# Output matmuls for two batches on a block-diagonal slot matrix, and small filler matmuls ahead of them, in a gated recurrence with a soft mixture of experts

## The chip, the cores and the metric

The kernel runs on one core of a Trainium2 chip. The metric is the device time of one execution in microseconds (us). A core has five engines that run at the same time, each with its own queue of instructions in program order: TensorE (PE in the profile; its loads of the stationary operand are the row PEld), VectorE (DVE), ScalarE (ACT), GpSimd (POOL) and SyncE (SP). TensorE writes to PSUM, eight banks of 2 KB per partition; other engines copy from there to SBUF, and DMA engines move data between SBUF and the memory (HBM). In this kernel SP issues the loads of the inputs and all stores, GpSimd the loads of the expert weights.

## What is computed

```python
def _attn_ref(x, f_logit, lower_bound):             # x, f_logit: 4 x 5056 x 256
    sig = 1.0 / (1.0 + np.exp(-f_logit))
    f = lower_bound[None, None, :] + (1.0 - lower_bound[None, None, :]) * sig
    i = 1.0 - f
    for t in range(S):
        h = f[:, t] * h + i[:, t] * x[:, t]
        y[:, t] = h

def _moe_ref(x, phi, w1, w2):                       # x: 20224 x 256, 8 experts with 4 slots each
    logits = x @ phi                                # 20224 x 32
    d = softmax over the tokens (logits)
    slot_input = d.T @ x                            # 32 x 256
    for e in range(E):
        h = np.maximum(slot_input[e] @ w1[e], 0.0)  # w1[e]: 256 x 1024
        slot_out[e] = h @ w2[e]                     # w2[e]: 1024 x 256
    c = softmax over the slots (logits)
    return c @ slot_out                             # 20224 x 256
```

The result of the recurrence is the token matrix of the mixture. No output row can be written before the last token of every batch has passed through the recurrence, because `slot_input` sums over all tokens. The output is 20224 x 256 in float32, 20.7 MB.

## The kernel before, in words

**First part, the recurrence (0 to about 134 us).** The 5056 tokens of a batch are cut into 10 groups of 512; a unit is one group of one batch, 40 in all. A unit is loaded, gated with a sigmoid (ScalarE), multiplied (GpSimd), transposed to channels (TensorE), scanned along the tokens (DVE, line 250), transposed back (line 263), and its logits against `phi` are taken. The exponentials of the logits stay in SBUF as `etall`: a tile of 128 partitions by 5056 tokens in bfloat16, where partitions 32b to 32b+31 hold the 32 slots of batch b. The order of the instructions is written out by hand; the framework adds the waits, and follows a tile for that, so that two parts of one tile may count as one.

**Second part, the experts (134 to 147 us).** TensorE is the only engine with much to do. In order: `slot_ps` is finished (lines 341 and 390); three matmuls of `spin` (line 130), which multiply the first 128 columns of `w1_sb[0]` with its first 512 columns into an unused bank, `tail[:, 1]`, and whose results nobody reads; four transposing matmuls of `slot_sb` (line 514); three more of `spin`; the first layer of the experts (line 544) into `hi_ps`; transposes of it (line 559); the second layer for experts 0 to 3 into `so4_ps` (line 580); then for experts 4 to 7 into `so_ps`, eight matmuls for each expert with `wide` as stationary operand (line 590). After the eight of expert 4 stand one matmul pair that adds `so4`, and the row sums (lines 324 and 327): 23 matmuls with a stationary part of `etall` and the four columns of `ones`, which give the denominators of the softmax over slots for the later blocks; DVE turns them into `rrow` (lines 600 and 601). The 24 matmuls of experts 5 to 7 follow. Line 602 then scales `so_ps` by `rcs` into `slot_out` (128 x 256, bfloat16; the rows of batch b again at partitions 32b to 32b+31, with the same 32 rows for all batches).

**Third part, the output (from 147 us).** The tokens of a batch are cut into `blocks`: two of 2048 tokens (16 rows of 128 partitions each), one of 896 (7 rows), and 64 left over that `rest` treats. For one row of one batch, `share` (line 620) makes one matmul: stationary is the part of `etall` with the 32 slots of this batch and 128 tokens, moving is `slot_out` with 256 columns.

```python
nc.tensor.matmul(op[:, j], ew[:, :, r + j], slot_out[ds(b * NS, NS), :],
                 start=True, stop=True, skip_group_check=True)
```

The result in PSUM (`op`, up to four rows of 256 columns, two banks) is scaled by `rrow` into `ob` in SBUF, in turn by DVE (`by_vector`, one instruction for four rows, line 610) and by ScalarE (`by_scalar`, one instruction a row, line 614). `pieces` does this for the first block of batch 0 in small parts, each stored as soon as it is ready (line 646); `whole` does a block of one batch and stores it with one DMA (line 657). The order is: `pieces` for block 0 of batch 0, `whole` for the block of 896 tokens for each batch, `rest`, then `whole` for the seven blocks of 2048 tokens. SP issues the stores in this order, and waits at each for the copies that fill it. `ob` is a pool of six buffers of 16 KB a partition, `op` one of four buffers of two banks.

Of the kernel before, what the change touches and what calls it, by code (L numbers as in the profile page):

```python
# [9 lines left out]
F32 = mybir.dt.float32  # L10
# [8 lines left out]
def kernel(  # L19
# [10 lines left out]
    nc = tc.nc  # L30
# [66 lines left out]
    for j in range(B // 2):  # L97
        nc.vector.memset(pair_ones[ds(j * 2 * NS, 2 * NS), ds(j, 1)], 1.0)

    def lb_constants():  # L100
        nc.vector.tensor_scalar(omlb, lb, -1.0, 1.0, ALU.mult, ALU.add)
        nc.vector.tensor_scalar(nomlb, lb, 1.0, -1.0, ALU.mult, ALU.add)
# [12 lines left out]
    nc.vector.memset(csum, 0.0)  # L115
    w1_r = moe_w1.rearrange("e (p o) f -> e p o f", o=DC)
    w2_r = moe_w2.rearrange("e (p fc) d -> e p fc d", p=P)
    w1_sb = [store.tile([P, DC, F], BF16, name=f"w1_sb{e}") for e in range(E)]
    w2_sb = [store.tile([P, FC, D], BF16, name=f"w2_sb{e}") for e in range(E)]

    def load_w(i):
        if i < E:
# [2 lines left out]
            nc.gpsimd.dma_start(out=w2_sb[i - E], in_=w2_r[i - E])  # L125


    def spin(dst, k):
        for _ in range(k):
            nc.tensor.matmul(dst, w1_sb[0][:, 0, :P], w1_sb[0][:, 0, :G],  # L130
                             start=True, stop=True, skip_group_check=True)

    W_AT = {9: 1, 15: 1, 21: 1, 27: 1, 31: 1, 33: 1, 34: 3, 35: 1, 36: 6}
    w_next = [0]
    ctx.enter_context(tc.manual_schedule())

    held = ExitStack()
    psu = held.enter_context(tc.tile_pool(name="psu", bufs=2, space=PSUM))
    psp = held.enter_context(tc.tile_pool(name="psp", bufs=1, space=PSUM))
    ld = held.enter_context(tc.tile_pool(name="ld", bufs=3))  # L140
    with tc.tile_pool(name="sp2", bufs=3) as sp2, \
# [271 lines left out]
        for n in range(n_unit):  # L413
            if n < SINGLE - 2:
                if n:
                    unit(to_tokens, n - 1)
                    unit(u_to_channels, n + 1)
                s_to_channels(n + 2)
                gate(n + 3, 1 if n + 3 < SINGLE else 2)
                decay(n + 2, 1)  # L420
                if n % 2 == 0:
                    unit(load, n + AHEAD)
                unit(enter, n + 3)
            else:
                end = n >= n_unit - 6
                if n % 2 == 0:
                    unit(load, n + AHEAD)
                    if n == SINGLE - 2:
                        to_tokens(n - 1)
                        keep_tokens(n - 1)  # L430
                    if not end:
                        unit(gate, n + 4)
                else:
                    unit(decay, n + 1)
                    if n == n_unit - 5:
                        gate(n + 3)
                        exps(odd - 1)
                if not end and n != n_unit - 7:
                    group(exps, n - 2)

                unit(enter, n + 3)
                for _ in range(W_AT.get(n, 0)):
                    load_w(w_next[0])
                    w_next[0] += 1

                if n == n_unit - 2:
                    unit(u_to_channels, n + 1)
                if n != SINGLE - 2:
                    unit(to_tokens, n - 1)
                if n == n_unit - 2:  # L450
                    keep_tokens(n - 1)
                if n % 2 == 0:
                    unit(s_to_channels, n + 2)
                    unit(s_to_channels, n + 3)
                if n != n_unit - 2:
                    unit(u_to_channels, n + 1)
                if n in (n_unit - 5, n_unit - 4):
                    idle(4)
                if n == n_unit - 2:
                    tail = psp.tile([P, 2, G], F32, name="tail", tag="sp")  # L460
                    rs_ps = tail[:, 0, ds(0, n_grp * R * B)].rearrange(
                        "p (q b) -> p q b", b=B)
                    late_ps, odd_ps = (
                        tail[:, 1].bitcast(BF16)[:, ds(i * R * P, R * P)].rearrange(
                            "p (r s) -> p r s", r=R) for i in range(2))
                    logits(odd)
                    exps(odd)
                    slots(odd - 1)
                    spin(tail[:, 1], 1)
                    odd_weights()  # L470
                elif not end:
                    group(logits, n - 1)
            if n == n_unit - 1:
                logits(last, [0, 1, 2])
                late_exps([0, 1, 2])
                row_sums(0)
                late_weights([0, 1, 2], nc.scalar.copy)

            unit(scan, n)
            if n == 0:  # L480
                rep_constants()
            if n not in (SINGLE - 2, n_unit - 2):
                unit(keep_tokens, n - 1)
            if n == n_unit - 3:
                weights_to_tokens(odd - 1)
                slots(odd - 2)
            elif not n >= n_unit - 6:
                group(weights_to_tokens, n - 3)
                batch(slots, n - 4, 0)
                batch(slots, n - 4, 1)  # L490
# [13 lines left out]
        slots(odd)  # L504
        late_slots([0, 1, 2])
        late_slots([3])
        spin(tail[:, 1], 3)
        slot_sb = hpool.tile([P, G, DC], BF16, name="slot_sb", tag="h")
        slot_sb = slot_sb.rearrange("p t o -> p (t o)").bitcast(F32)[:, ds(0, D)]
        nc.vector.tensor_copy(slot_sb, slot_ps)  # L510
# [3 lines left out]
            nc.tensor.matmul(sin_ps[:, o], slot_v[:, o], rep[:, 0],  # L514
                             start=True, stop=True, skip_group_check=True)

    slot_out = store.tile([P, D], BF16, name="slot_out")
    with tc.tile_pool(name="ew", bufs=1) as ew, \
         tc.tile_pool(name="pm", bufs=2, space=PSUM) as pm, \
         tc.tile_pool(name="pbig", bufs=1, space=PSUM) as pbig:  # L520

        rep2 = rep.rearrange("p b s -> p (b s)")

        spin(tail[:, 1], 3)
        sin = ew.tile([P, DC, NS], BF16, name="sin")
        nc.vector.tensor_scalar_mul(sin[:, 0], sin_ps[:, 0], omlb[:, ds(0, 1)])
        nc.scalar.activation(sin[:, 1], sin_ps[:, 1], ACT.Copy, scale=omlb[:, ds(1, 1)])
# [24 lines left out]
            his.append(hi)  # L552
        cs_ps = pm.tile([P, 1], F32, name="cs_ps", tag="pm")
        rcs = ew.tile([P, 1], F32, name="rcs")
        for q in range(E // Q):
            ht_ps = psu.tile([P, FC, P], BF16, name="ht_ps", tag="up")
            hi_v = his[q].rearrange("p (c f) -> p f c", f=FC)
# [2 lines left out]
            if q == 0:  # L560
                nc.tensor.matmul(cs_ps, rep2, cs1, start=True, stop=True)
                src = ht_ps.rearrange("p f (j s) -> p f j s", s=NS)[:, :, :, ds(0, SPE)]
                src = bass.AP(tensor=src.tensor, offset=src.offset,
                              ap=[list(src.ap[0]), [P, FC], [NS + SPE, Q], [1, SPE]])
                dst = hid[:, :, :, ds(0, SPE)]
                dst = bass.AP(tensor=dst.tensor, offset=dst.offset,
                              ap=[list(dst.ap[0]), [Q * NS, FC], [NS + SPE, Q], [1, SPE]])
                nc.scalar.copy(dst, src)
                nc.vector.reciprocal(rcs, cs_ps)
                continue  # L570
            for j in range(Q):
                s0 = (Q + j) * SPE
# [15 lines left out]
        for j in range(Q):  # L588
# [5 lines left out]
            if j == 0:  # L594
                nc.tensor.matmul(so_ps, rep2, so4, start=False, stop=False,
                                 skip_group_check=True)
                for i in range(1, len(blocks)):
                    row_sums(i)
                q = n_grp * R - 1
                nc.vector.reciprocal(rrow[:, wide_r:q], rs_ps[:, wide_r:q])  # L600
                nc.vector.reciprocal(rrow[:, q, ds(0, B // 2)], rs_ps[:, q, ds(0, B // 2)])
        nc.vector.tensor_scalar_mul(slot_out, so_ps, rcs)


    held.close()
    with tc.tile_pool(name="pout", bufs=4, space=PSUM) as pout, \
         tc.tile_pool(name="osb", bufs=6) as osb:

        def by_vector(ob, op, scale):
            nc.vector.tensor_tensor(ob, op, scale.broadcast_to(list(ob.shape)), ALU.mult)  # L610
# [5 lines left out]
        def share(op, i, b, r, k):  # L616
            t0, n_r = blocks[i]
            ew = etall[ds(b * NS, NS), ds(t0, P * n_r)].rearrange("s (p r) -> s p r", r=n_r)
            for j in range(k):
                nc.tensor.matmul(op[:, j], ew[:, :, r + j], slot_out[ds(b * NS, NS), :],  # L620
                                 start=True, stop=True, skip_group_check=True)

        def scale_of(i, b, r, k):
# [24 lines left out]
        def whole(i, b):  # L648
# [7 lines left out]
                by(ob[:, ds(r, k)], op[:, ds(0, k)], scale_of(i, b, r, k))  # L656
            nc.sync.dma_start(out=rows_of(i, b), in_=ob)

        def rest():
            n_p = B // 2  # L660
            op = pout.tile([P, R, D], F32, name="op", tag="op")
            ob = osb.tile([P, n_p, D], F32, name="ob", tag="ob")
            for j in range(n_p):
                k = ds(j * 2 * NS, 2 * NS)
                nc.tensor.matmul(op[:, j * R // n_p], left[k].rearrange("s t u -> s (t u)"),
                                 slot_out[k, :], start=True, stop=True, skip_group_check=True)
            by_vector(ob, op.rearrange("p (j k) d -> p k j d", j=n_p)[:, 0],
                      rrow[:, n_grp * R - 1, ds(0, n_p)].unsqueeze(2))
            dst = out.rearrange("(b t) d -> t b d", b=B)
            for j in range(n_p):  # L670
                nc.sync.dma_start(out=dst[ds(S - L, L), ds(2 * j, 2)], in_=ob[:, j])

        end = len(blocks) - 1
        pieces(0, 0, [(1, 2), (3,), (2,)])
        for b in range(B):
            whole(end, b)
        rest()
        for i in range(end):
            for b in range(B):
                if i or b:  # L680
                    whole(i, b)


# [28 lines left out]
```

## Time and profile before

| what | value |
|---|---|
| median of 12 runs | 203.84 us (203.2 to 205.33) |
| profiled execution | 203.79 us, span 202.0 us |
| busy in the span | PE 130.9, DVE 144.6, ACT 137.2, POOL 99.2 us |
| read and written | 58.23 MB read, 20.71 MB written, 391 GB/s over the span |
| mean granted TensorE clock | 0.836 |
| output matmuls, line 620 | 156, of 32x128 stationary and 256 moving columns |
| output copies | ACT line 614: 76, mean 491 ns; DVE line 610: 23, mean 1104 ns |
| stores of 2 MB | 7, median 15.9 us from issue to landing |

The span runs from the first to the last instruction of the profiled execution; the time of the execution is 1.79 us longer. Busy times of engines overlap, so they don't add up to the span. A matmul's own duration in the profile contains its way through the array, and neighbours overlap; what one costs in a row of many is the distance between them. The row "PEclk" gives the clock that TensorE was granted in tenths of full speed (9 is 90% or more).

### The profile page before, as it was taken

The numbers are of one execution on the slowest core, as the hardware profiler recorded it, in microseconds if no ns is written. First come the engines' busy times: TensorE is split into PE (matmuls) and PEld (weight loads), VectorE is DVE, ScalarE is ACT, GpSimd is POOL, SyncE is SP. The second block draws the span as 40 slices with busy tenths as digits, with TensorE's granted clock in tenths as the row PEclk, the third lists the DMA queues.
The fourth block names the chain that finished last, engine by engine and source line by source line (L and its number), as shares of the span: only waits on it lengthen the run. The fifth ranks groups of instructions, "written<-read, shape, count | busy, mean of one in ns | idle before, by whom it ended". The sixth has DMA issues, their size and how long they took to land.

```text
span 202.0 us, 3056 instructions
## 1 busy us (share of the span) xinstructions
PE 130.9 (65%) x1097; PEld 102.0 (50%) x1097; DVE 144.6 (72%) x162; ACT 137.2 (68%) x193; POOL 99.2 (49%) x70
## 2 busy tenths in 40 slices
PE   0586473874976658584976776999989999910000
PEld 0365342754864556564766555665965766700000
DVE  1699888698799999979998799915268887710000
ACT  2688664899988999599996498434069799940000
POOL 2588585893979469952995859950000000000000
PEclk9999999699699999879997999999985555555555
DMA  6999999999999999999999999999539999999993
GB/s 176 416 406 413 406 412 408 404 414 309 416 409 380 345 414 407 321 409 396 390 310 406 324 245 211 213 212 217 110 135 397 421 422 435 422 415 428 444 425 162
DMA packets 17614, 70.74 MB, mean 350 GB/s; under 512 B 2096, under 2 KB 3120, under 8 KB 16704
## 3 DMA queue, kind: packets, MB, share of 16 engines
q1 hardware_dynamic: 15120, 62.13, 76.8%
q0 software_dynamic: 2336, 8.42, 20.7%
q8 instruction: 8, 0.13, 0.2%
q14 instruction: 6, 0.05, 0.1%
q10 hardware_dynamic: 144, 0.00, 0.0%
HBM read 58.23 MB, written 20.71 MB: 391 GB/s over the span
## 4 chain that ended last, share of the span: by engine, by line
PE 30%; DVE 26%; DMA 15%; ACT 9%; issue 7%; SPq 1%; ACTq 0%; DVEq 0%
DVE h L250 20%; DMA f_t<-in_f_logit_dram 11%; PE op L620 9%; ACT ob L614 5%; PE hp L263 5%; DVE ht L277 4%; DMA x_t<-in_x_dram 4%; PE sp L217 4%; PE so_ps L590 2%; ACT s_t L191 2%; PE up L217 2%; PE tail L324 1%; SPq L181 1%; PE slot_ps L341 1%; PE hi_ps L544 1%
## 5 line engine op out<-in xcount | busy, mean ns | idle before, releaser
L202 POOL TENSOR_TENSOR u_t<-s_t,x_t 128x1024 bf16<-128x1024 bf16 (+1 forms) x39 | 82.4, 2130 | 29.9 <-ACT s_t L191 22.4
L250 DVE TENSOR_TENSOR_SCAN h<-a,h,up 128x512 bf16<-128x512 f32 (+1 forms) x72 | 86.4, 1250 | 6.2 <-PE up L217 3.8
L263 PE MATMUL hp<-ident_f,h 128*128 128x128 f32 (+1 forms) x160 | 31.2, 322 | 32.8 <-DVE ht L277 19.8
L191 ACT ACTIVATE s_t<-f_t 128x2048 bf16<-128x2048 f32 (+2 forms) x23 | 38.4, 1670 | 16.0 <-DMA f_t<-in_f_logit_dram 15.9
L240 ACT ACTIVATE a<-sp,nomlb 128x1024 f32<-128x1024 bf16 (+2 forms) x46 | 43.3, 993 | 3.5 <-PE sp L217 1.9
L263 PEld LDWEIGHTS hp<-ident_f,h 128*128 128x128 f32 (+1 forms) x160 | 23.1, 208 | 42.7 <-DVE ht L277 24.5
L614 ACT ACTIVATE ob<-op,rrow 128x256 f32<-128x256 f32 x76 | 28.6, 491 | 8.9 <-PE op L620 8.5
L217 PE MATMUL sp<-ident_f,s_t 128*128 128x128 f32 x144 | 23.9, 315 | 9.6 <-ACT s_t L191 6.1
L620 PE MATMUL op<-slot_out,etall 32*128 32x256 bf16 x156 | 28.2, 400 | 1.9 <-ACT ob L614 0.9
L610 DVE TENSOR_TENSOR ob<-op,rrow 128x1024 f32<-128x1024 f32 (+3 forms) x23 | 24.4, 1104 | 5.8 <-PE op L620 4.5
L217 PEld LDWEIGHTS sp<-ident_f,s_t 128*128 128x128 f32 x144 | 19.8, 164 | 11.1 <-issue 6.0
L620 PEld LDWEIGHTS <-etall 32*128 32x128 bf16 x156 | 20.2, 154 | 9.5 <-issue 4.5
L217 PE MATMUL up<-ident_f,u_t 128*128 128x128 f32 x144 | 24.0, 292 | 0.6 <-POOL u_t L202 0.6
L217 PEld LDWEIGHTS up<-ident_f,u_t 128*128 128x128 f32 x144 | 18.7, 154 | 1.8 <-POOL u_t L202 1.0
L277 DVE COPY ht<-hp 128x512 f32<-128x512 f32 (+1 forms) x22 | 14.8, 670 | 3.1 <-PE hp L263 3.0
L277 ACT COPY ht<-hp 128x512 f32<-128x512 f32 (+1 forms) x18 | 10.4, 576 | 4.9 <-PE hp L263 4.9
L250 DVE TENSOR_TENSOR_SCAN h<-a,up 128x512 bf16<-128x512 f32 x8 | 9.3, 1207 | 0.7 <-PE up L217 0.7
L291 PE MATMUL lg<-h,phi 128*32 128x512 bf16 (+1 forms) x80 | 6.9, 391 | 0.0
L341 PE MATMUL slot_ps<-ht,et 128*32 128x256 bf16 (+1 forms) x144 | 5.7, 277 | 0.8 <-DVE et L315 0.8
L191 ACT ACT_TABLE_LOAD x4 | 5.1, 1283 | 1.2 <-PEq L696 1.2
L300 ACT ACT_TABLE_LOAD x4 | 5.1, 1283 | 0.1
L300 ACT ACTIVATE etall<-lg 128x1024 bf16<-128x1024 f32 (+1 forms) x5 | 4.6, 927 | 0.0
(88 smaller groups left out, 90.0 us busy)
## 6 DMA issues: line engine op xcount, KB each, us to landing
f_t<-in_f_logit_dram SPq DMA_DIRECT2D x36, 512.0 KB, 10.5
x_t<-in_x_dram SPq DMA_DIRECT2D x36, 512.0 KB, 10.7
out_dram<-ob SPq DMA_DIRECT2D x7, 2048.0 KB, 15.9
w_sb<-in_moe_w_dram POOLq DMA_DIRECT2D x16, 512.0 KB, 8.4
out_dram<-ob SPq DMA_DIRECT2D x4, 896.0 KB, 7.9
f_t<-in_f_logit_dram SPq DMA_DIRECT2D x4, 384.0 KB, 7.7
x_t<-in_x_dram SPq DMA_DIRECT2D x4, 384.0 KB, 7.4
out_dram<-ob SPq DMA_DIRECT2D x4, 256.0 KB, 3.8
```

Source lines behind the costliest of these rows:

```text
L191: nc.scalar.activation(s_t, f_t, ACT.Sigmoid, scale=-1.0)
L202: nc.gpsimd.tensor_tensor(uts[n][:, :r], s_t[:, :r], x_t[:, :r], ALU.mult)
L217: nc.tensor.transpose(ps[:, :, r], t[:, r], ident_f)
L240: nc.scalar.activation(decays[n // 2, o][:, ds(n % 2, k), :T], sp[:, ds(n % 2, k), :T, o], ACT.Identity, scale=nomlb[:, ds(o, 1)], bias=1.0)
L250: nc.vector.tensor_tensor_scan(h[:, :T, o], decays[n // 2, o][:, n % 2, :T], up[:, :T, o], hs[n - B][:, ds(used(n // B - 1) - 1, 1), o] if ...
L263: nc.tensor.transpose(hp[:n_p, r], hw[:, :n_p, r], ident_f)
L277: copy(hts[g][:n_p, b].rearrange("p r d -> p (r d)").bitcast(F32), hps.pop(n)[:n_p].rearrange("p r c -> p (r c)"))
L300: nc.scalar.activation(etall[:, ds(first(gs[0]), T)], lgs[0][:, :T], ACT.Exp, accum_out=csum[:, ds(g, 1)])
L341: nc.tensor.matmul(slot_ps[ds(b * NS, NS), :], et[:n_p, r, b], ht[:n_p, b, r], start=(g == 0 and r == 0), stop=(g == n_grp - 1 and r == R ...
L610: nc.vector.tensor_tensor(ob, op, scale.broadcast_to(list(ob.shape)), ALU.mult)
L614: nc.scalar.activation(ob[:, i], op[:, i], ACT.Copy, scale=scale[:, i])
L620: nc.tensor.matmul(op[:, j], ew[:, :, r + j], slot_out[ds(b * NS, NS), :], start=True, stop=True, skip_group_check=True)
```

## The change

It has four parts.

1. `slot_out` becomes `slot_bd` (128 x 2 x 256). In column half 0 only the rows of even batches are filled, in half 1 only those of odd batches; the other rows are zero. This is done by scaling `so_ps` with two columns, `rcs2`, which are `rcs` times `parity` (0 or 1). DVE writes the even half, ScalarE the odd half.
2. A new function `couple` makes the output of two batches at once. One matmul has 64 partitions as stationary operand (the slots of two batches for the same 128 tokens) and 512 moving columns, the output of one batch in each half, one PSUM bank. DVE copies two rows of two batches with one instruction, ScalarE with four. Both batches lie in one buffer of SBUF, `oc`, and are stored with one DMA each when both are complete. `couple` takes the place of `whole` except for block 0 of batch 1, and `rest` adds the two halves of its product.
3. The weights `w1_sb` and `w2_sb` move into a pool that is closed before the output, so that its space is free for `oc` (three buffers of 32 KB) beside `ob` (three of 16 KB).
4. `spin` takes its width as an argument. The two groups of 3 matmuls with 512 columns become groups of 12 with 128 columns. A new group of 25 with 32 columns stands after the row sums, ahead of the last 24 matmuls of `so_ps`.

```diff
+    parity = consts.tile([P, 2], F32, name="parity")
+    nc.vector.memset(parity, 0.0)
+    for b in range(B):
+        nc.vector.memset(parity[ds(b * NS, NS), ds(b % 2, 1)], 1.0)
...
+    slot_bd = store.tile([P, 2, D], BF16, name="slot_bd")
+    held = ExitStack()
+    wts = held.enter_context(tc.tile_pool(name="wts", bufs=1))
+    w1_sb = [wts.tile([P, DC, F], BF16, name=f"w1_sb{e}") for e in range(E)]
+    w2_sb = [wts.tile([P, FC, D], BF16, name=f"w2_sb{e}") for e in range(E)]
...
-    def spin(dst, k):
+    def spin(dst, k, w):
         for _ in range(k):
-            nc.tensor.matmul(dst, w1_sb[0][:, 0, :P], w1_sb[0][:, 0, :G],
+            nc.tensor.matmul(dst[:, ds(0, w)], w1_sb[0][:, 0, :P], w1_sb[0][:, 0, :w],
                              start=True, stop=True, skip_group_check=True)
+    SPINS = 25
...
-        spin(tail[:, 1], 3)
+        spin(tail[:, 1], 12, P)
         slot_sb = hpool.tile([P, G, DC], BF16, name="slot_sb", tag="h")
...
-        spin(tail[:, 1], 3)
+        spin(tail[:, 1], 12, P)
         sin = ew.tile([P, DC, NS], BF16, name="sin")
...
                 nc.vector.reciprocal(rcs, cs_ps)
+                nc.vector.tensor_scalar_mul(rcs2, parity, rcs)
...
                 for i in range(1, len(blocks)):
                     row_sums(i)
                 q = n_grp * R - 1
+                spin(tail[:, 1], SPINS, NS)
                 nc.vector.reciprocal(rrow[:, wide_r:q], rs_ps[:, wide_r:q])
                 nc.vector.reciprocal(rrow[:, q, ds(0, B // 2)], rs_ps[:, q, ds(0, B // 2)])
-        nc.vector.tensor_scalar_mul(slot_out, so_ps, rcs)
+        nc.vector.tensor_scalar_mul(slot_bd[:, 0], so_ps, rcs2[:, ds(0, 1)])
+        nc.scalar.activation(slot_bd[:, 1], so_ps, ACT.Copy, scale=rcs2[:, ds(1, 1)])
...
-         tc.tile_pool(name="osb", bufs=6) as osb:
+         tc.tile_pool(name="osb", bufs=3) as osb:
...
-                nc.tensor.matmul(op[:, j], ew[:, :, r + j], slot_out[ds(b * NS, NS), :],
+                nc.tensor.matmul(op[:, j], ew[:, :, r + j], slot_bd[ds(b * NS, NS), b % 2],
                                  start=True, stop=True, skip_group_check=True)
...
+        def couple(i, j):
+            t0, n_r = blocks[i]
+            ew = etall[ds(j * 2 * NS, 2 * NS), ds(t0, P * n_r)].rearrange(
+                "s (p r) -> s p r", r=n_r)
+            scale = rrow[:, ds(t0 // P, n_r), ds(2 * j, 2)]
+            ob = osb.tile([P, 2, n_r, D], F32, name="oc", tag="oc")
+            for t, r in enumerate(range(0, n_r, 2)):
+                k = min(2, n_r - r)
+                op = pout.tile([P, 2, 2, D], F32, name="op", tag="op")
+                for i_r in range(k):
+                    nc.tensor.matmul(op[:, i_r].rearrange("p u d -> p (u d)"),
+                                     ew[:, :, r + i_r],
+                                     slot_bd[ds(j * 2 * NS, 2 * NS)].rearrange("s u d -> s (u d)"),
+                                     start=True, stop=True, skip_group_check=True)
+                if t % 2 == 0:
+                    nc.vector.tensor_tensor(
+                        ob[:, :, ds(r, k)].rearrange("p u r d -> p r u d"), op[:, ds(0, k)],
+                        scale[:, ds(r, k)].unsqueeze(3).broadcast_to([P, k, 2, D]), ALU.mult)
+                else:
+                    for i_r in range(k):
+                        for u in range(2):
+                            nc.scalar.activation(ob[:, u, r + i_r], op[:, i_r, u], ACT.Copy,
+                                                 scale=scale[:, r + i_r, ds(u, 1)])
+            for u in range(2):
+                nc.sync.dma_start(out=rows_of(i, 2 * j + u), in_=ob[:, u])
...
         pieces(0, 0, [(1, 2), (3,), (2,)])
-        for b in range(B):
-            whole(end, b)
+        couple(end, 0)
+        couple(end, 1)
         rest()
+        whole(0, 1)
         for i in range(end):
-            for b in range(B):
-                if i or b:
-                    whole(i, b)
+            for j in range(B // 2):
+                if i or j:
+                    couple(i, j)
```

## The prediction

> **What bounds the kernel now.** I read the 40 slices of the page first, then the stretches by microsecond around the place where the traffic changes from loads to stores, then the instructions in order of time there, and last the built order of the changed kernel, for the waits that the diff does not show.
>
> From the page, the clock, the DMA share and the rate, in slices of 5.05 us:
>
> ```profile
> PEclk9999999699699999879997999999985555555555
> DMA  6999999999999999999999999999539999999993
> GB/s 176 416 406 413 406 412 408 404 414 309 416 409 380 345 414 407 321 409 396 390 310 406 324 245 211 213 212 217 110 135 397 421 422 435 422 415 428 444 425 162
> ```
>
> The DMA engines are full except in slices 28 and 29 (141 to 151 us): the weights have landed and no store has begun. After that they are full until the last store. The same place by microsecond (busy time of each engine, then clock, DMA share, GB/s):
>
> ```profile
> 143.00:144.00 1.00, 1.00 (x20) 1.00 (x20) 0.00 (x0) 0.00 (x0) 0.00 (x0) 1.00 0.80 164
> 144.00:145.00 1.00, 1.00 (x15) 0.92 (x14) 0.64 (x1) 0.00 (x0) 0.00 (x0) 1.00 0.29 57
> ...
> 146.00:147.00 1.00, 0.96 (x9) 0.72 (x8) 0.00 (x0) 0.00 (x0) 0.00 (x0) 1.00 0.00 0
> ...
> 149.00:150.00 1.00, 1.00 (x9) 0.90 (x8) 1.00 (x2) 1.00 (x3) 0.00 (x0) 0.77 0.66 214
> 150.00:151.00 1.00, 1.00 (x8) 0.64 (x8) 0.88 (x2) 1.00 (x4) 0.00 (x0) 0.50 0.75 269
> 151.00:152.00 1.00, 1.00 (x10) 0.81 (x10) 0.62 (x1) 0.61 (x2) 0.00 (x0) 0.50 1.06 394
> ...
> 178.00:198.00 20.00, 0.00 (x0) 0.00 (x0) 0.00 (x0) 0.96 (x3) 0.00 (x0) 0.50 1.01 428
> ```
>
> So there are two stages. From about 144 to 149 us the DMA engines are empty, and TensorE's chain alone decides when the first store can go. From 151 to 198 us the stores decide: 20.7 MB at about 425 GB/s are 49 us, and from 178 us on the engines have nothing left to do but two last copies. A microsecond added to TensorE's chain before the first store therefore comes out at the end, whole. A microsecond saved in the output matmuls comes out as nothing unless the stores starve. TensorE's chain in that gap:
>
> ```profile
> 142.83 1.47 PE L324 MATMUL tail<-ones,etall 128*128 128x4 bf16 x23
> ...
> 144.18 2.78 PE L590 MATMUL so_ps<-w_sb,wide 128*128 128x256 bf16 x24
> ...
> 147.00 0.48 DVE L602 TENSOR_SCALAR slot_out<-so_ps,rcs 128x256 bf16<-128x256 f32 x1 [1.89 <-PE so_ps L590]
> ...
> 147.54 0.37 PE L620 MATMUL op<-slot_out,etall 32*128 32x256 bf16 x2 [0.58 <-DVE slot_out L602]
> ...
> 148.40 4.96 SPq L646 DMA_DIRECT2D out_dram<-ob  x8
> ```
>
> Nothing waits in it: 24 matmuls in 2.78 us are 116 ns each, so the last weights are not late.
>
> **The 25 fillers.** They stand in TensorE's order between the row sums (L324) and the last 24 matmuls of `so_ps` (L590), so each of them delays `slot_out`. Nothing covers them. The nearest row is L324: the same stationary size (128x128 bf16, one load each), 4 moving columns where a filler has 32; 23 in 1.47 us are 64 ns each, so 25 cost 1.60 us. From above, the 128-column transposes L559 (8 in 0.68 us, 85 ns) give 2.1 us. From below, L390 (16 with a 32-column stationary in 0.45 us, 28 ns) gives 0.7 us. I take 1.60, since the stationary load is the same. The reciprocal at L600, now behind them on DVE, would end near 146 us and is needed only after `so_ps`.
>
> Here the Trainium skill can be weighed (TensorE: Matmul & The Clock Gate, Back-to-back issue gap). It gives small matmuls a floor of about 25 ns from start to start, or about 62 ns where the sequencer's firmware decodes them; the sum would be 0.63 us by the one and 1.55 us by the other. The 64 ns of L324 side with the second.
>
> **The two older spins, 3x512 columns becoming 12x128.** The same columns, four times the loads. Both stand on the path:
>
> ```profile
> 134.61 0.82 PE L130 MATMUL tail<-w_sb 128*128 128x512 bf16 x3
> 134.74 0.42 DVE L510 COPY slot_sb<-slot_ps 128x256 f32<-128x256 f32 x1 [0.73 <-PE slot_ps L390]
> ...
> 135.27 0.61 PE L514 MATMUL tail<-rep,slot_sb 128*128 128x32 f32 x4
> ...
> 135.72 0.81 PE L130 MATMUL tail<-w_sb 128*128 128x512 bf16 x3
> ...
> 136.64 0.25 DVE L526 TENSOR_SCALAR sin<-tail,omlb 128x32 bf16<-128x32 f32 x1 [1.47 <-PE tail L130]
> ```
>
> The first covers the copy of `slot_sb`, ready at 135.16, but by the chain of waits holds TensorE from 134.68 to 135.43. The second holds `sin`, by the releaser in brackets, although `sin` needs only L514. By the 85 ns of L559, which also has 128x128 stationary and 128 moving columns, 12 take 1.02 us. The first then ends at 135.70, 0.27 later; the second takes 1.02 instead of 0.66, 0.36 more. Together 0.63 us. If the loads hide wholly, at a quarter of the present 220 ns, it is nothing; at 100 ns each it is 1.0 us. I take 0.63.
>
> **`slot_bd`.** DVE writes the even half, 128x256 as `slot_out` was (0.48 us), and ScalarE the odd half. In the built order the ScalarE half waits for DVE, and the first output matmul, which reads only the even half, waits for ScalarE. So the two are in series. The trace shows the same alternation where two engines share one PSUM tile: the four `wide` copies at L575 start at 140.67, 140.97, 141.23 and 141.52, ScalarE and DVE in turn, each when the other has ended. Price: one 128x256 activation from PSUM, L614's 0.47 us, plus a handover of about 0.03: 0.50 us, between 0.40 (the spacing of such activations) and 0.55. A rule of the Trainium skill speaks against this part too (PSUM — Partial Sum Buffer, Terms): two engines are not to be at one bank and quadrant at once, reads included, so by it these halves could not overlap even with other waits.
>
> **Parts that cost nothing.** The `parity` memsets (five of about 0.1 us) lie on DVE before 5.04 us, where it idles 3.43 us for `lb`; without that cover, 0.4. `rcs2` (0.17 us, by L101) lies in DVE's 0.86 us of idling before the first `wide` copy; without the cover it costs its 0.17.
>
> **The output stage.** Sizes and order of the stores are unchanged: 2 MB in pieces, four of 896 KB, the rest, seven of 2 MB. Copies are the same in number and shape, 76 activations, apart from three short ones in `rest`. Of the 156 stationary loads about half go, and moving columns stay: a half-clock matmul of 256 columns takes 197 ns (40 in 7.89 us), 512 should take about 0.4. Compute was 20 us ahead of the stores, so this gives nothing at the end. Buffers: three of 32 KB and three of 16 KB for six of 16 KB, so nothing waits longer on a store; the first write into the weights' place needs only matmuls that had to end anyway. One thing worsens: the first pair is issued when both batches are done. The first 896 KB store went at 153.48, 5.1 us after the first piece; the pair needs seven more blocks of 0.2 us less some overlap, so about 6.2 us. The pieces run out 6.6 us after the first issue (2.04 MB have moved by 155.0), and a store takes some 0.6 us to start, so a hole of up to 0.5 us is possible. Against it, dense matmuls now end later and the clock may stay whole during the pieces, where stores starve: 0.3 us back. I take zero for both.
>
> **Sum.** 1.60 + 0.63 + 0.50 = 2.73 us. The profiled execution took 203.79 us (span 202.0 and 1.79 around it), 0.05 under the median of 203.84. So 206.5 us.
>
> **Rivals.** *The clock falls in the longer thin stretch.* The clock changes on a grid: half from 36.9 to 40.3, from 108.6 to 112.0, and from 149.53 on; each spell of the first two is 3.4 us, and these dates differ by multiples of that. The stretch 146.1 to 149.5, with TensorE at 2.42 of 3.40 us and much of it on 32 rows, was followed by half clock. Row sums and fillers together make 3.1 us in which hardly any columns move. If a grid period holds most of it, the 24 L590 matmuls run at 197 instead of 116 ns; 17 fit in 3.4 us, so 1.4 us more: 207.9. Against it: TensorE counts as busy throughout. On the clock the skill states (TensorE: Matmul & The Clock Gate, Part 1) that one busy window of 3.4 us brings the full clock. By that no drop would come and the sum stays 206.5; but TensorE is busy for all of 155 to 165 us here, at half clock.
>
> *Cheap fillers.* If fillers cost 28 ns and the loads of the spins hide, 0.70 + 0 + 0.50 give 205.0. For it: the stationary never changes. Against it: it is loaded each time, and L324 shows 64 ns.
>
> *Faster.* The full clock lasts through the pieces and 64-row matmuls bring it back afterwards, so the stores never starve and compute leaves the memory sooner. By 151 us 0.49 MB had moved, where 393 GB/s from 149 would give 0.79: 0.75 us to win. The stores run at 424 GB/s beside compute and 428 without it, under 0.3 us more. At most 1.05 us, so about 203.4 if the additions cost 0.6. It decides only if additions stay below some 0.4 us, which needs the first two terms near nothing; ScalarE's half alone is 0.5.
>
> *No change.* If additions of about 1.1 us meet that gain, 203.9. It needs both low ends at once.
>
> **How the numbers follow.** The sum as it stands 0.62, the clock 0.17, cheap fillers 0.11, no change 0.04, faster 0.06. The range leaves out the last two and half of the tails: 205.2 (1.4 above now: fillers low, a little of the spins) to 208.0 (with the clock's price). About 0.3%, or 0.6 us, is what a measurement here tells from no change: faster 0.06, same 0.04, slower 0.90.
>
> **What would show it.** First store at about 151.1 instead of 148.40, with the DMA share at nothing for some 7 us; fillers at 60 to 70 ns; the spins near 1.0 us each; ScalarE's `slot_bd` after DVE's and the first output matmul after both; store rate and the time from first store to the end as before. I am wrong if the first store is not later, if the fillers end before something that TensorE had to wait for anyway, or if first store to end changes by over 0.7 us.

## The result, and the profile after

The changed kernel takes 202.62 us (median of 12 runs, 200.92 to 203.44). Against the kernel before, run beside it, the ratio is 0.9912, with a 95% interval of 0.9888 to 0.9936: 1.8 us faster. I had forecast 206.5 and gave "faster" 6 in 100. The profiled execution took 202.79 us, its span is 201.0.

First the three rows of the 40 slices again, of the changed kernel:

```profile
PEclk9999999699799988999997999999996555555555
DMA  6999999999999999999999999999419999999994
GB/s 186 418 418 420 422 423 413 418 418 314 420 415 371 363 419 415 319 413 411 410 314 404 272 210 212 214 210 214 95 56 411 425 421 453 427 417 430 453 421 212
```

The gap in slices 28 and 29 is there, deeper than before, as forecast. Outside it something differs that I had not asked about: with the DMA share at 9 in both kernels, most slices of the loads carry 413 to 423 GB/s where they carried 404 to 416.

By microsecond, in the columns of the earlier table (busy time and count of PE, PEld, DVE, ACT and POOL, then clock, DMA share, GB/s):

```profile
144.00:145.00 1.00, 1.00 (x20) 0.92 (x17) 0.67 (x2) 0.00 (x0) 0.00 (x0) 1.00 0.00 0
...
149.00:150.00 1.00, 1.00 (x10) 0.97 (x9) 0.74 (x2) 0.52 (x3) 0.00 (x0) 1.00 0.29 98
150.00:151.00 1.00, 0.87 (x6) 0.65 (x5) 1.00 (x2) 1.00 (x4) 0.00 (x0) 1.00 0.67 242
151.00:152.00 1.00, 1.00 (x5) 0.49 (x4) 0.92 (x2) 1.00 (x4) 0.00 (x0) 1.00 1.04 399
152.00:153.00 1.00, 1.00 (x5) 0.36 (x4) 0.96 (x2) 1.00 (x4) 0.00 (x0) 0.55 1.07 427
178.00:198.00 20.00, 1.22 (x3) 0.16 (x1) 1.23 (x1) 2.68 (x8) 0.00 (x0) 0.50 1.00 430
```

The clock holds until 152.1 us instead of 149.5. TensorE's chain ahead of the stores, from the instructions in order of time (line numbers moved: L332 was L324, L138 was L130, L599 was L590):

```profile
133.90 0.84 PE L138 MATMUL tail<-w_sb 128*128 128x128 bf16 x12
...
135.02 0.83 PE L138 MATMUL tail<-w_sb 128*128 128x128 bf16 x12
...
142.16 1.47 PE L332 MATMUL tail<-ones,etall 128*128 128x4 bf16 x23
...
143.52 0.78 PE L138 MATMUL tail<-w_sb 128*128 128x32 bf16 x25
...
144.14 2.78 PE L599 MATMUL so_ps<-w_sb,wide 128*128 128x256 bf16 x24
...
146.96 0.48 DVE L612 TENSOR_SCALAR slot_bd<-so_ps,rcs 128x256 bf16<-128x256 f32 x1 [1.87 <-PE so_ps L599]
147.54 0.47 ACT L613 ACTIVATE slot_bd<-so_ps,rcs 128x256 bf16<-128x256 f32 x1 [6.71 <-DVE slot_bd L612]
148.07 0.37 PE L631 MATMUL op<-slot_bd,etall 32*128 32x256 bf16 x2 [1.14 <-ACT slot_bd L613]
...
148.87 4.51 SPq L657 DMA_DIRECT2D out_dram<-ob  x8
```

The additions can be read off, with the help of the chain of waits. First its lines of the spins in the kernel before, then of spins and fillers in the changed one:

```profile
134.68 0.76 PE tail L130 x3
...
135.88 0.66 PE tail L130 x3
```

```profile
133.97 0.78 PE tail L138 x12
...
135.19 0.68 PE tail L138 x12
...
143.66 0.64 PE tail L138 x25
```

The fillers begin at 143.52 and the next matmuls at 144.14; on the chain the 25 cost 0.64 us, about 25 ns each from start to start. `slot_bd` is in series: from the start of DVE's half to the first output matmul 1.11 us, before 0.54, so 0.57. The spins are nearly unchanged: 0.78 and 0.68 us, before 0.76 and 0.66. That is 1.25 us more, yet the first store is issued at 148.87, only 0.47 after the 148.40 of before. So 0.8 us came from the time before the experts. And from that issue to the end of the span it takes 52.1 us, before 53.6: another 1.5 us.

The part of the page on DMA queues gives the first lead (packets, MB, share of the span of 16 engines). The kernel before, then the changed one:

```profile
q1 hardware_dynamic: 15120, 62.13, 76.8%
```

```profile
q1 hardware_dynamic: 15120, 62.13, 75.8%
```

The same packets and bytes, but they take 0.768 x 202.0 = 155.1 us of each of the 16 engines in the mean, against 0.758 x 201.0 = 152.4. (This product is called the packets' time below.) The queue became 2.7 us cheaper, though the change leaves the number and the size of its packets alone. In the trace most packets of this queue take the same time in the changed kernel: 16 KB 0.611 us, 7 KB 0.272, 4 KB loads 0.159 (medians, and over the whole span the 90th percentiles too). Before, the 16 KB packets are at 0.615 in the median, with 0.627 as the 90th percentile; the 4 KB loads from 20 to 60 us are at 0.162, with 0.167.

### The profile page after: what moved, and what is told of

The parts are those of the page before. It is cut to its first block, busy times and chain, and to the rows that moved or that the text cites. A ratio compares the mean times of both kernels' runs of the same rounds, so it can differ in the third digit from the quotient of the medians.

```text
span 201.0 us, 3018 instructions
## 1 busy us (share of the span) xinstructions
PE 133.5 (66%) x1078; PEld 96.7 (48%) x1078; DVE 146.4 (73%) x169; ACT 138.9 (69%) x195; POOL 99.1 (49%) x70
## 4 chain that ended last, share of the span: by engine, by line
PE 37%; DVE 26%; DMA 15%; issue 6%; ACT 4%; SPq 1%; ACTq 0%; DVEq 0%
DVE h L258 20%; PE op L680 12%; DMA f_t<-in_f_logit_dram 11%; PE hp L271 5%; DVE ht L285 4%; DMA x_t<-in_x_dram 4%; PE sp L225 4%; PE op L631 2%; PE up L225 2%; ACT s_t L199 2%; PE so_ps L599 2%; PE slot_ps L349 2%; PE tail L138 1%; PE tail L332 1%; SPq L189 1%
## 5 line engine op out<-in xcount | busy, mean ns | idle before, releaser
L225 PE MATMUL sp<-ident_f,s_t 128*128 128x128 f32 x144 | 23.4, 311 | 9.3 <-ACT s_t L199 5.9
L680 PE MATMUL op<-slot_bd,etall 64*128 64x512 bf16 x62 | 24.4, 602 | 0.1
L691 ACT ACTIVATE oc<-op,rrow 128x256 f32<-128x256 f32 x60 | 22.7, 488 | 1.5 <-PE op L680 0.9
L685 DVE TENSOR_TENSOR oc<-op,rrow 128x1024 f32<-128x1024 f32 x16 | 19.3, 1222 | 4.6 <-PE op L680 4.5
L680 PEld LDWEIGHTS <-etall 64*128 64x128 bf16 x62 | 9.1, 154 | 14.0 <-issue 11.7
L625 ACT ACTIVATE ob<-op,rrow 128x256 f32<-128x256 f32 x16 | 6.3, 479 | 1.9 <-PE op L631 1.8
L631 PE MATMUL op<-slot_bd,etall 32*128 32x256 bf16 x32 | 5.9, 340 | 1.5 <-ACT slot_bd L613 1.1
L349 PE MATMUL slot_ps<-ht,et 128*32 128x256 bf16 (+1 forms) x144 | 6.2, 295 | 0.8 <-DVE et L323 0.8
L631 PEld LDWEIGHTS <-etall 32*128 32x128 bf16 x32 | 4.3, 148 | 3.5 <-issue 1.8
```

What stands on the lines that cost most here:

```text
L225: nc.tensor.transpose(ps[:, :, r], t[:, r], ident_f)
L349: nc.tensor.matmul(slot_ps[ds(b * NS, NS), :], et[:n_p, r, b], ht[:n_p, b, r], start=(g == 0 and r == 0), stop=(g == n_grp - 1 and r == R ...
L631: nc.tensor.matmul(op[:, j], ew[:, :, r + j], slot_bd[ds(b * NS, NS), b % 2], start=True, stop=True, skip_group_check=True)
L680: nc.tensor.matmul(op[:, i_r].rearrange("p u d -> p (u d)"), ew[:, :, r + i_r], slot_bd[ds(j * 2 * NS, 2 * NS)].rearrange("s u d -> s (u d)"),
L685: nc.vector.tensor_tensor(ob[:, :, ds(r, k)].rearrange("p u r d -> p r u d"), op[:, ds(0, k)], scale[:, ds(r, k)].unsqueeze(3).broadcast_t ...
L691: nc.scalar.activation(ob[:, u, r + i_r], op[:, i_r, u], ACT.Copy, scale=scale[:, r + i_r, ds(u, 1)])
```

## The experiments

Theory: `parity`, the new constant, takes 32 bytes of each partition ahead of all large buffers that a DMA touches. In the built programs all buffers of `f_t`, `x_t` and `ob` begin 224 bytes past a multiple of 256 before, and on a multiple of 256 after, `oc` too. Rival: the output for two batches, with the clock held longer by the fillers, feeds the stores better.

**The kernel before once more.** To see whether the slow packets are of the kernel or of one execution.

> The kernel before once more, unchanged, for a second profile. Placement theory (the new 32-byte tile parity moves the SBUF buffers of all DMAs from 224 bytes past a multiple of 256 to a multiple of 256): the slow packets belong to the program, so they are there again: the hardware queue's 15120 packets take about 155 us of the 16 engines (76.8% of 202.0 in the first profile), 152.4 in the changed kernel (75.8% of 201.0). Output theory (matmuls for two batches and the longer full clock feed the stores better): the packets' time says nothing of the kernel; it may be anywhere between 152 and 156. Time: 0.0% against before by both.

Ratio 1.0006 (0.9971 to 1.0040). Its packets take 0.764 x 202.2 = 154.5 us: they are slow again.

**The 32 bytes alone.**

```diff
+    pad = consts.tile([P, 8], F32, name="pad")
     pair_ones = consts.tile([P, B // 2], BF16, name="pair_ones")
```

> The kernel before with 32 unused bytes a partition ahead of the other constants, nothing else. Placement theory: 2.5 to 2.9 us faster than before (the fall of the packets' time from 155.1 to 152.4), so about 201.4, and 1 us faster than the changed kernel, since it has neither the 25 fillers (0.64 us) nor ScalarE's half of slot_bd (0.5 us); packets near 152.4 us. Output theory: no change, within 0.3 us of before.

Ratio 0.9922 (0.9889 to 0.9955), 202.24 us: an unused tile is worth 1.6 us. The direction decides between the theories; the size is 1 us under what I had expected. The page of this kernel, its queue (152.3 us), and a stretch of the loads before (first fence below) and with the 32 bytes (second):

```profile
span 200.4 us, 3056 instructions
...
q1 hardware_dynamic: 15120, 62.13, 76.0%
```

```profile
20.00:60.00 40.00, 25.72 (x212) 21.18 (x211) 33.51 (x33) 31.62 (x30) 28.99 (x15) 0.91 1.03 397
```

```profile
20.00:60.00 40.00, 28.16 (x220) 22.75 (x219) 34.65 (x34) 32.75 (x30) 30.13 (x16) 0.87 1.03 405
```

The same DMA share, 1.03, moves 405 instead of 397 GB/s, and every engine is busy for longer in the same 40 us, though the mean clock is lower.

**The changed kernel with 32 bytes more** (the same line, in the changed kernel), so that its buffers begin 32 bytes past a multiple of 256.

> The changed kernel with 32 unused bytes a partition ahead of the constants, so that all its DMA buffers start 32 bytes past a multiple of 256. Placement theory: it loses the gain and keeps the additions of 0.64 + 0.52 us, so 0.8 to 1.3 us slower than before, about 205.3; packets at 155 us. Output theory: as the changed kernel, 1.6 us faster than before.

Ratio 0.9995 (0.9958 to 1.0031). The gain is gone, and packets take 0.767 x 202.1 = 155.0 us:

```profile
span 202.1 us, 3018 instructions
...
q1 hardware_dynamic: 15120, 62.13, 76.7%
```

But I had expected it 0.8 to 1.3 us slower than before, for the additions; it is as fast. So something beside placement pays for them.

**Other offsets**, 96 and 160 unused bytes in the kernel before, which put the buffers 64 and 128 bytes past a multiple of 256.

> The kernel before with 96 unused bytes: all DMA buffers start 64 bytes past a multiple of 256. If a multiple of 64 is enough, 0.8% under before and packets at their floor (152 us of the 16 engines); if only 256 will do, as before, packets at 155.

> The kernel before with 160 unused bytes: all DMA buffers start 128 bytes past a multiple of 256. If a multiple of 64 or 128 is enough, 0.8% under before and packets at 152 us; if only 256 will do, as before, packets at 155.

Ratios 0.9985 (0.9956 to 1.0015) and 0.9989 (0.9954 to 1.0023), packets 154.5 and 154.8 us. Neither 64 nor 128 will do. The Trainium skill (DMA: Bandwidth & Descriptors, How a descriptor splits into AXI transactions) says that a transaction of a transfer has to start at an address that is a multiple of 256 bytes, and that a descriptor which does not begin there starts at the multiple below, with bytes that are fetched and not used. The five offsets here agree as far as that multiple goes: 0 is fast, 32, 64, 128 and 224 are slow. That the unused bytes are the reason no run here shows.

**What pays for the additions: the fillers?**

```diff
-    SPINS = 25
+    SPINS = 0
```

> The changed kernel without the group of 25 fillers. If fillers only delay slot_out: 0.6 us faster than the changed kernel (2.2 to 2.4 us faster than before), first store 0.64 us earlier after the end of the row sums. If they pay by keeping the clock full for the first stores: as the changed kernel or slower.

Ratio 0.9947 (0.9916 to 0.9978): it is not faster than the changed kernel, and more likely slower. Its stores show why. After the first microseconds the DMA engines stand empty:

```profile
149.50:150.00 0.50, 0.49 (x3) 0.26 (x2) 0.42 (x1) 0.50 (x2) 0.00 (x0) 0.84 0.96 369
150.00:150.50 0.50, 0.50 (x2) 0.28 (x2) 0.50 (x1) 0.39 (x2) 0.00 (x0) 0.50 0.47 176
150.50:151.00 0.50, 0.50 (x4) 0.28 (x2) 0.30 (x1) 0.50 (x2) 0.00 (x0) 0.50 0.03 4
151.00:151.50 0.50, 0.50 (x4) 0.15 (x1) 0.32 (x1) 0.50 (x3) 0.00 (x0) 0.50 0.06 12
```

SP's own instructions in that stretch:

```profile
148.93 2.28 SPq L657 DMA_DIRECT2D out_dram<-ob  x1
```

Issuing a store takes SP 0.33 to 0.5 us for most of the other pieces (0.84 us for the last); this one took 2.28. In the same time, from 149.07 on, one 16 KB packet of queue 8 (kind "instruction") takes 1.76 us; among the loads such packets take 0.9 to 1.1. It goes with TensorE's program: in the eight profiles so far the last of these packets begins after 1977 to 1998 records of TensorE (weight loads, matmuls and waits), whatever the time, which is near the 1500th instruction of TensorE's built program. Where in that program the first output matmul stands decides where the packet falls: it is the 1417th instruction before, with the packet at 155.05, among the stores; the 1453rd without fillers, at 149.07; the 1503rd in the changed kernel, at 146.62, in the empty gap. So the new theory: the fillers, and the splitting of the spins, move a code packet out of the stores. Rival, still: they hold the clock.

**Small matmuls far from the output.** The function below, called in the recurrence, adds two instructions a matmul to TensorE's program where it has time.

```diff
+        def tiny(k):
+            for _ in range(k):
+                nc.tensor.matmul(slot_bank[:, 1, ds(0, NS)], ident, ident[:, ds(0, NS)],
+                                 start=False, stop=False, skip_group_check=True)
...
+                if n in range(14, 25):
+                    tiny(5)
```

In the kernel before with the 32 bytes, 55 of them:

> The kernel before with the 32 unused bytes, and 55 small matmuls (128x128 stationary, 32 columns, result unread) spread over units 14 to 24 of the recurrence, so that TensorE's program is 110 instructions further on when the output begins. Code-fetch theory (TensorE's code comes in 16 KB packets on queue 8, one of which falls among the stores at 153 to 155 us before, at 1.5 and 4.4 us after the first store, and in the empty time before the first store in the changed kernel): the packet now falls near 145 us, the last DMA engine no longer ends 1.2 to 1.5 us after the others, and the time is 0.9 to 1.4 us under the kernel with the 32 bytes alone (202.24), so about 201.1, 1.4% under before. Clock theory (only matmuls right before the output help, by keeping the clock full): no faster than 202.2, or slower by what the small matmuls cost in the recurrence.

Ratio 0.9948 (0.9922 to 0.9974): a miss. The packet did fall in the gap, at 144.44 us; but with 110 instructions more the next one, near the 1760th, now fell at 170.50, again among the stores, and the last engine was as late as ever. The kernel before makes 158 output matmuls, over 310 instructions, more than the 260 or so between two packets, so it can't do without a packet there; the output for two batches makes 96, under 200.

With 18 of them (3 in each of units 14 to 19):

> The same with 18 small matmuls, 36 instructions, which puts the code packet where the changed kernel without fillers has it, some 2 us after the first store. Code-fetch theory: the issue of a store by SP stalls for about 2 us there and the stores have a hole of 1.4 us, so it is as slow as or slower than the 32 bytes alone: 202.2 to 203.3. If the hole belonged to the output for two batches, there would be none here.

Ratio 0.9959 (0.9930 to 0.9989), against 0.9922 with the 32 bytes alone; the intervals overlap. The profile has the packet at 149.54 (1.51 us long), an issue of SP that takes 1.54 us from 149.89 on, and a thin half microsecond. The hole is smaller than the 1.4 us of the kernel without fillers, but it comes with the packet, and without the output for two batches. This kernel has one more packet at 176.73, and two DMA engines that end late (share 0.15 from 198 to 199 us), so its time does not price the first packet alone.

In the changed kernel without fillers, 25 of them (5 in each of units 14 to 18):

> The changed kernel with the 25 fillers moved out of the gap into units 14 to 18 of the recurrence; the count of instructions ahead of the output is the same. Code-fetch theory: the packet still falls before the first store, nothing is lost, and the 0.64 us of the fillers are saved: about 0.5 us under the changed kernel, 1.1% under before. Clock theory: as without fillers, 0.5% under before, with thin stores in the first microseconds.

Ratio 0.9911 (0.9881 to 0.9941), the same as with the fillers in the gap, where I had expected 0.2% less. Nothing stands before the last 24 `so_ps` matmuls now, and the stores have no hole: fillers next to the output are not needed. That the 0.64 us don't show in the ratio is possible within the two intervals.

And 75 of them (5 in each of units 14 to 28), which differs from the run before only in 100 instructions:

> The changed kernel without fillers in the gap, and 75 small matmuls in units 14 to 28 of the recurrence instead of 25, so that TensorE's program is 100 instructions further on when the output begins. From the other runs a 16 KB code packet comes near instruction 1760 (170.5 us and 176.7 us in the two kernels before with early matmuls); here that lies among the stores, near 170 us. Code-fetch theory: one DMA engine is about 1 us behind the others at the end, and the time is 0.8 to 1.2 us over the kernel with 25 early matmuls: 0.4 to 0.5% under before instead of 0.9%. If code packets are hidden among the stores: as with 25.

Ratio 0.9947 (0.9910 to 0.9984), packet at 167.99. That is 0.7 us more than with 25, but the two intervals overlap; the profiles are clearer. The end of the stores with 25 (first fence) and with 75 (second), by half microseconds, last column but one the DMA share:

```profile
197.50:198.00 0.50, 0.00 (x0) 0.00 (x0) 0.00 (x0) 0.00 (x0) 0.00 (x0) 0.50 1.22 524
198.00:198.50 0.50, 0.00 (x0) 0.00 (x0) 0.00 (x0) 0.00 (x0) 0.00 (x0) 0.50 0.09 33
198.50:199.00 0.50, 0.00 (x0) 0.00 (x0) 0.00 (x0) 0.00 (x0) 0.00 (x0) 0.50 0.00 0
```

```profile
196.00:196.50 0.50, 0.00 (x0) 0.00 (x0) 0.00 (x0) 0.00 (x0) 0.00 (x0) 0.50 1.15 492
196.50:197.00 0.50, 0.00 (x0) 0.00 (x0) 0.00 (x0) 0.00 (x0) 0.00 (x0) 0.50 0.17 66
197.00:197.50 0.50, 0.00 (x0) 0.00 (x0) 0.00 (x0) 0.00 (x0) 0.00 (x0) 0.50 0.08 33
197.50:198.00 0.50, 0.00 (x0) 0.00 (x0) 0.00 (x0) 0.00 (x0) 0.00 (x0) 0.50 0.08 33
```

A share of 0.08 is about one engine of 16: with the code packet among the stores, fifteen engines are done about a microsecond before the last one. The stage from the first store's first byte to the last byte, from the packets of each profile:

| kernel | offset to 256 | code packet (16 KB) among the stores | stage, us |
|---|---|---|---|
| before; again; 96 bytes; 160 bytes | 224; 224; 64; 128 | yes | 51.2; 51.1; 51.0; 51.3 |
| changed, 32 bytes more | 32 | no | 50.1 |
| before with 32 bytes; with 55 early | 0 | yes | 50.9; 50.9 |
| changed, 75 early | 0 | yes | 50.9 |
| changed | 0 | no | 49.5 |
| changed, 25 early | 0 | no | 49.5 |
| before with 18 early; changed without fillers | 0 | yes, about 2 us after the first store, with a hole | 51.1; 51.2 |

By these single profiles the packet costs 1.4 us of the stage on aligned buffers and about 1.0 on the others; alignment is worth 0.6 without the packet.

The same profiles speak against the rival of the clock. In the kernel with 160 unused bytes the clock stayed full until 3.6 us after the first store was issued, in the kernel before until 1.1 us after it, and the stages are 51.3 and 51.2 us. In the changed kernel it is 3.2 us. So a full clock of that length needs no fillers, and it is not what shortens the stage.

**Beyond both kernels.** From the changed kernel with 25 early matmuls on: DVE writes `slot_out` as before, which `share` reads again, so that the first output matmul has one wait, and GpSimd makes `slot_bd` of it:

```diff
-        nc.vector.tensor_scalar_mul(slot_bd[:, 0], so_ps, rcs2[:, ds(0, 1)])
-        nc.scalar.activation(slot_bd[:, 1], so_ps, ACT.Copy, scale=rcs2[:, ds(1, 1)])
+        nc.vector.tensor_scalar_mul(slot_out, so_ps, rcs)
+        for u in range(2):
+            nc.gpsimd.tensor_scalar_mul(slot_bd[:, u], slot_out, parity[:, ds(u, 1)])
```

> The same, and DVE writes slot_out as before; GpSimd makes slot_bd of it (two products with parity), so that the first output matmul no longer waits for ScalarE's half. By the traces another 0.5 us less: about 1.4% under before, as the kernel before with 32 bytes and 55 early matmuls if the output for two batches in itself is worth nothing; lower by what it is worth.

Ratio 0.9866 (0.9831 to 0.9902), 201.26 us. Its profile has a hole, though, before the first pair of blocks is stored; here the clock had fallen at 148.07:

```profile
153.00:153.50 0.50, 0.50 (x2) 0.22 (x2) 0.50 (x2) 0.38 (x2) 0.00 (x0) 0.50 1.00 389
153.50:154.00 0.50, 0.50 (x3) 0.23 (x3) 0.50 (x1) 0.26 (x1) 0.00 (x0) 0.50 0.03 8
154.00:154.50 0.50, 0.50 (x4) 0.22 (x2) 0.29 (x1) 0.50 (x3) 0.00 (x0) 0.50 1.09 459
```

So the last kernel makes the first two blocks of 896 tokens one by one, in two buffers of their own:

```diff
-        couple(end, 0)
+        whole(end, 0)
+        whole(end, 1)
         couple(end, 1)
```

> The kernel with slot_out from DVE, slot_bd from GpSimd and 25 early matmuls, in which the 896-token blocks of batches 0 and 1 are made one after the other again, with buffers of their own, before the pairs. In that kernel's profile the first pair was issued 6.1 us after the first store, and the stores had a hole of 0.5 us there. Expected: first 896 KB store about 5 us after the first store, no hole, 0.3 to 0.5 us less: 1.5% under before. If the hole costs nothing: 1.3%.

Ratio 0.9854 (0.9806 to 0.9903), median 201.62, span of the profile 199.3. The first block of 896 KB is issued at 151.80, 4.6 us after the first store, the hole is gone, and the stage takes 49.5 us instead of 50.0. In the runs this can't be told from the kernel ahead of it.

## Why the prediction was wrong, point by point

**What bounds the kernel** was right: the DMA engines stand empty ahead of the first store, and are full after it. From it I drew that the time after the first store could not change as long as sizes and order of the stores did not. That step failed: from the first issue to the end it took 52.1 us instead of 53.6, and the stage from first to last byte 49.5 instead of 51.2. The bytes were the same; the time of a packet was not, nor was what else used the same DMA engines. The first store came only 0.47 us later, where I had added up 2.73: the additions were 1.25, and the time before the experts became 0.8 shorter.

**"Parts that cost nothing"** is where the largest term was lost. I priced `parity` by its five memsets and not by its 32 bytes. They are worth 0.8% in both directions, 1.6 us: 0.9922 where they are added alone, and from 0.9912 to 0.9995 where their effect is undone. The sum had no term for the place of a buffer. That these 32 bytes end on a multiple of 256 is luck: nothing in the change aims at it.

**The output stage** was to give nothing at the end. It gave about 1.0 to 1.4 us, by the stage times above, and not for any reason that I weighed: fewer output matmuls are fewer instructions, and together with the instructions added ahead of them the code packet came before the stores and no further one after it. That too is luck. By the runs the size is less sure: the changed kernel off the multiple was 0.1 us faster than before in spite of additions of 1.25, which makes 1.35, with 0.75 on either side; 75 against 25 early matmuls make 0.7, with intervals that overlap.

**The 25 fillers**: 1.60 us forecast, 0.64 measured. I misread the row that I chose, L324: its 1.47 us hold the last matmul's own way through the array; from its first start to the start of the next matmul it is 1.33 us (142.83 to 144.16), 58 ns each, which would have made 1.45. And it was the wrong row. It has the same size of stationary operand, but reads it from `etall` with a stride, every 16th or 7th element; the fillers read theirs contiguously. Within the row the matmuls with stride 16 start 62 ns apart and those with stride 7 start 53 to 54 ns apart, the fillers 25. That fits the stride as the reason; it was not tried alone. The floor of 25 ns that the Trainium skill states (TensorE: Matmul & The Clock Gate, Back-to-back issue gap) was the better price: 25 ns here. I had set it aside for the row. **The spins**: 0.63 forecast, 0.04 measured; the loads do hide, at 56 ns from start to start. The 85 ns of L559 and the 116 ns of L590 hold the same way through the array; from start to start they are mostly 60 to 63 and 109. Both terms came out at or just under the low ends that I had written down.

**ScalarE's half of `slot_bd`**: 0.50 forecast, 0.57 measured, in the order that I had read from the built program. Taking the wait out moved the ratio from 0.9911 to 0.9866, within what the two intervals leave open; the profile of that kernel has DVE's `slot_out` directly ahead of the matmul.

**The hole before the first pair**: forecast as up to 0.5 us, set to zero. In the changed kernel the pair was issued 5.2 us after the first store, with a full clock for 3.2 of them, and there is no hole; in the kernel with GpSimd's `slot_bd`, where the clock fell 1.0 us after the first store, the pair came after 6.1 us and the hole was 0.5 us. From its issue to its first packet the first store took 0.84 us before and 0.85 after, where I had put 0.6.

**Rivals.** The clock did not fall ahead of `so_ps`; it held longer. The grid of 3.4 us that I read stands, though the kernel before has two more spells at half clock than I named, from 50.55 and from 84.68 us. *Faster* had the right sign by the wrong mechanism: in the first 4 us after the first byte the DMA engines were idle for 0.40 us instead of 0.41, so feeding them better was worth next to nothing, not 0.75.

The sum that the runs support, for the changed kernel: additions 0.64 + 0.04 + 0.57 = 1.25 us; code packet and its late engine -1.0 to -1.4; placement -1.6. That is -1.3 to -1.8, and the ratio says -1.8 with an interval of about 0.5 on either side. The additions and the packet are read from single profiles, the placement from runs.

What stays open: how far the first store moves by placement alone. Its date, less the additions, was 147.8 to 149.1 in the profiles off the multiple of 256 (median 148.4) and 146.1 to 148.7 in those on it (median 147.2); the scatter of single profiles is as wide as the step, and only the ratios carry it. Nor was it tried which of loads and stores gains how much.

## What to carry to other kernels

Where DMA engines are full, look up where the buffers begin in SBUF before reasoning about the work: a constant of 32 bytes at the front can shift all of them, and multiples of 256 bytes were needed here. Compare the time of the same packets in two profiles (share of the queue times span) before looking for a cause among instructions. And count the instructions of the busiest engine ahead of a DMA-bound stage: its code comes over the same DMA engines, so padding or shortening its program can move a packet into, or out of, the part that sets the end.

## What the hardware showed that I had not expected

- From 20 to 60 us, the 4 KB packets to SBUF of the input loads took 0.159 us in the median on a multiple of 256 and 0.162 at 224 bytes past it (0.160 against 0.163 in the mean); 16 KB packets from SBUF 0.611 against 0.615, and 0.62 in the mean while engines worked beside them. Offsets of 32, 64 and 128 were as slow in the sum. The 4 KB packets of the weight loads that GpSimd issues took 0.324 us in the median in both kernels, though their buffers moved by the same 32 bytes.
- One 16 KB packet of code among the full stores takes about 0.95 us of one DMA engine and, by the profiles, delays the end of all by 1.0 to 1.4 us. Twice an issue of SP was held up in its company, by 1.1 and 1.9 us.
- Back-to-back matmuls of 32 columns with the same contiguous stationary, loaded each time, went at 25 ns from start to start, and with 128 columns at 56 ns, while those of 4 columns with a strided stationary went at 62 ns (stride 16) and 53 to 54 ns (stride 7).
- TensorE counted as busy for the whole of 156 to 178 us and stayed at half clock, with matmuls of 64 rows; before, with 32 rows, it was busy for 20.5 of these 22 us, at half clock too.
